# Attention, MoE and a second feed-forward layer in one program: weight conversions carried past the attention's last step

## The chip, the cores and the metric

The program runs on one core of a Trainium2 chip. The metric is the device time of one execution in microseconds; 446.7 us is the median of three runs of the kernel before (446.63 to 448.39). TensorE (PE) multiplies matrices, VectorE (DVE), ScalarE (ACT) and GpSimd (POOL) work on tiles, and SyncE (SP) issues most transfers. Each engine executes its instructions in program order. Waits between them are semaphores.

## What is computed

The reference runs three stages, one behind the other: banded attention with block summaries, a mixture of experts with one expert a token (top 1, with a capacity), and a feed-forward layer with an ELU.

```python
scores_l = scale * q @ k.T                 # masked to |i - j| < 16
scores_s = scale * q @ block_max(k).T + log(32)
a = softmax(concat(scores_l, scores_s))    # B=2, H=8, S=768, D=64
x = a @ concat(v, block_mean(v))           # -> 1536 tokens x 512

expert = argmax(x @ w_gate)                # 8 experts
h = relu(disp[expert] @ w1[expert])        # 512 -> 1024
x = gate * (h @ w2[expert])                # 1024 -> 512

h = x @ w_in                               # 512 -> 2048, w_in and w_out in float64
out = where(h > 0, h, exp(min(h, 0)) - 1) @ w_out
```

## The kernel before

**Attention.** 12 tiles of 128 tokens times two groups of heads make 24 steps, n = 0 to 23 (loop in `moe_chain_kernel`). A step runs `stage_s` (scores, L535 to L542 on PE), `stage_x` (maximum L554, negated L559 and exponentials L566), `stage_t` (transposition of the step before, L583), `stage_o` (product with v two steps back, L594, and its scaling L605). The gate of each tile (`gate_1` to `gate_6`) follows some steps behind, through the lists EARLY, MID and LATE. It ends in `put`, an indirect DMA on POOL (L718) that writes the tile's 128 rows to their expert's place in the DRAM tensor `xdisp`. The place is in `idx` (L688 on POOL, L685 on DVE for the last two tiles), of which there are two buffers. `late(n)` (L800 and on) holds what a step does besides: key windows for the next tile (`put_ks`, L450 on POOL), loads, clearing.

**Tail.** The tuple `tail` finishes the gates of the last tiles, then a few small operations make the lists of work units (`lists_i`, L990), from which SP reads addresses.

**The first unit beside it.** The first expert unit, e0, is chosen from token 0. Its 384 rows are read back early: `load_rows(XROW0)` at n = 20 (SP). The generator `first_unit` transposes them (`split_x`, four pieces of three transposes at L271, a cast on ACT at L272, a subtraction on DVE at L273), then runs 24 groups of four matmuls (L260), and then the second layer (L280). `fill_pe(n)` advances it by n pieces. `point()` reads the next entry of POINTS: the tens are pieces for `fill_pe`, the units are steps taken from `conv_tail`. `rest_of_first` runs what is left of the first unit; it starts the second layer and loads the second unit's weights and rows.

**Conversions.** w_in and w_out come as float64 in 32 chunks of 128x512 numbers (512 KB). A chunk's conversion is three DVE instructions (L405, L408, L399; called steps 1, 2 and 3 here). Chunks 8 to 13 have buffers of their own. The others, in order, share a ring of three. Step 3 of a chunk issues the load of the chunk three further on in the ring (`conv_next`), on SP's queue. Chunk 7 is loaded when chunk 4 is done, chunk 6 when chunk 3 is, 14 behind 5, 15 behind 6, 16 behind 7. In the attention, chunks 0 to 6 are queued in `pieces` from n = 10 on, one chunk every second step; `fill_in()` takes one step of them in each `stage_x` and one more in each odd `stage_o`. At n = 23 what is left in `pieces` is drained in one go (L910). Chunks 7 to 10 stand in `conv_tail`, are taken by `point()`, and what is left is drained behind the lists (L1005).

```python
            if n == NST - 1:
                while pieces:
                    fill_in()
```

Two regions of `xdisp` are cleared by SP from `fill_row`: e0's own rows at n = 8 (L840) and the spare rows behind all experts at n = 4 (L819).

Of the kernel before, what the change touches and what calls it, by code (L numbers as in the profile page):

```python
# [13 lines left out]
U32 = mybir.dt.uint32  # L14
# [12 lines left out]
E, F = 8, 1024  # L27
FF = 2048
P = 128
# [82 lines left out]
def moe_chain_kernel(  # L112
# [104 lines left out]

    puts = []
    pieces = []

    def load_rows(xr, row, queue=nc.sync):
        for s in range(NS):
# [115 lines left out]


    NCHUNK = 32  # L340
    CONV_ATT = 7
    CONV_FROM = 10
    CONV_LOAD = 7
    W_FROM = 9
    W_AT = (9, 11, 13, 15, 17, 19, 21, 23)
    X_AT = 20
    A_AT = (15, 21)
    POINTS = (0, 0, 0, 0, 11, 1, 0, 0, 30, 0, 1, 11, 0, 1, 0, 22, 0, 22, 0, 30, 10, 10, 0, 0, 10, 0, 10, 0, 0, 0, 0, 20, 40, 50)
    WARM = 23
    PROLOGUE = 2  # L350
    Y_AT = 4
    B_AFTER = (4, 7)
    H_AFTER = (0, 2, 7)
    CONV_TAIL = 4
    CONV_LATE = 3
    CONV_UNIT = (2, 8, 8)
    X_TILE = 6
# [63 lines left out]
    with ExitStack() as att:  # L421
# [105 lines left out]
        def fill_in():  # L527
            if pieces:
                pieces.pop(0)()
# [142 lines left out]
        def gate_4(i):  # L672
            gp, oh, r, s, el, nmx, xr = st.pop(("g3", i))
            rk = gp[:, E : 2 * E]
            nc.tensor.matmul(rk, tri_b, oh, start=True, stop=(i == 0))
            if i > 0:
                nc.tensor.matmul(rk, ones_b, ohs[i - 1], start=False, stop=True)
            t1, rank, row, ob = sm("t1", E), sm("rank"), sm("row"), sm("ob")
            idx = sm("idx", 1, U32)
            en = nc.vector if i >= last - 1 else nc.gpsimd  # L680
            en.tensor_scalar(row, r, -float(REG), float(E * REG), op0=ALU.mult, op1=ALU.add)
            nc.vector.scalar_tensor_tensor(t1, rk, 1.0, oh, op0=ALU.mult, op1=ALU.mult, accum_out=rank)
            en.tensor_scalar(ob, rank, cap, float(OOB), op0=ALU.is_ge, op1=ALU.mult)
            if i >= last - 1:
                nc.vector.scalar_tensor_tensor(idx, rank, row, ob, op0=ALU.add, op1=ALU.add)  # L685
            else:
                en.tensor_tensor(row, row, rank, op=ALU.add)
                en.tensor_scalar(idx, row, ob, None, op0=ALU.add)  # L688
            if i < last - 1:
                nc.scalar.activation(el, gp[:, 0:E], AF.Exp, bias=nmx, accum_out=s)  # L690
            st["g4", i] = (idx, xr, s)
# [94 lines left out]


        points = iter(POINTS)
        conv_tail = [step for i in range(CONV_ATT, CONV_ATT + CONV_TAIL) for step in conversion(i)]

        def point():
            n, conv = divmod(next(points, 0), 10)
# [5 lines left out]
        def late(n):  # L798

            i = 1 if n == 0 else (n + 3) // 2  # L800
            if (n == 0 or n % 2 == 1) and i < NTT:
                new_kw(i)
                put_ks(i, nc.gpsimd.tensor_copy)
                put_kw(i, nc.vector.tensor_copy)
            if n == 0:
                nc.sync.dma_start(wg, w_gate.rearrange("p (k e) -> p k e", e=E))
                nc.sync.dma_start(cap_raw, capacity.to_broadcast([P, 1]))
                nc.vector.tensor_copy(tri_b, C("tri"))
                nc.vector.memset(ones_f, 1.0)
            if n == 1:  # L810
                nc.gpsimd.memset(fill_row, 0.0)
                nc.gpsimd.tensor_copy(fill_row[:, DM:].bitcast(U32), C("oob").bitcast(U32))
                nc.gpsimd.tensor_copy(oobs, C("oob")[:, 0:1].bitcast(U32).to_broadcast([P, REG // P]))  # L813
                nc.vector.tensor_copy(cap, cap_raw.bitcast(I32)[:, 0:1])
            if n in (2, 4):
                load_k(1, n - 2, 2)
            if n == 4:
                nc.sync.dma_start(ids.rearrange("(p a) o -> p (a o)", a=REG // P), oobs)
                nc.sync.dma_start(xdisp[E * REG :, :].rearrange("(s p) d -> p s d", p=P), fill)  # L819
            if 5 <= n < 5 + KD:  # L820
                block_max(1, n - 5)
            if n % 2 == 0 and n // 2 + 2 < NTT:
                load_q(n // 2 + 2)
            if n % 2 == 1 and (n - 1) // 2 + 2 < NTT:
                load_vx((n - 1) // 2 + 2)
            if n in (3, 5, 6, 7):
                load_vt(1, (3, 5, 6, 7).index(n))
            if 6 <= n < 10:
                block_sums(1, n - 6, nc.gpsimd)
            if n == 11:  # L830
                block_means(vts.pop(1))
            if 11 <= n < 11 + NVX:
                put_means(n - 11)
            if n == 7:
                nc.vector.tensor_scalar(e0_i, r0[0:1], -1.0, float(E), op0=ALU.mult, op1=ALU.add)
            if n == 16:
                unit_order()
            if n == W_FROM - 1:
                e0 = st["e0"] = nc.sync.value_load(e0_i, min_val=0, max_val=E - 1)
                nc.sync.dma_start(xdisp[ds(e0 * REG, SLOT), :].rearrange("(s p) d -> p s d", p=P), fill)  # L840
            if n == W_FROM + 1:
                put(0)
            if n >= W_FROM:
                if n == X_AT:
                    nc.gpsimd.tensor_copy(oh32[:, 1], oh_x.unsqueeze(2).to_broadcast([P, E, NCH]))
                    load_rows(XROW0, st["e0"] * REG)
                load_w(st["e0"], [m for m, at in zip(W_ORDER, W_AT) if n == at])
            if n in A_AT:
                round_a(A_AT.index(n), W1_RAW[A_AT.index(n)])
            if n == CONV_LOAD:  # L850
                for m in range(len(RAW)):
                    conv_load(m)
            if n == NST - 2:
                for m in AHEAD[0:4]:
                    conv_load(m)
            if n >= CONV_FROM and conv[0] < CONV_ATT and n % 2 == 0:
                pieces.extend(conversion(conv[0]))
                conv[0] += 1
# [19 lines left out]
        for n in range(NST):  # L878
# [29 lines left out]
            if at(2):  # L908
                stage_o(*at(2))
            if n == NST - 1:  # L910
                while pieces:
                    fill_in()
            if n >= NST - 2:
                point()
            for gate, i in LATE.get(n, ()):
# [20 lines left out]
        for gate, *at in tail:  # L936
            gate(*at)
            if gate is rest_o and at[1]:
                held["acc"] = False

                for m in AHEAD[4:]:
                    conv_load(m)
            point()


# [56 lines left out]
        nc.vector.tensor_reduce(last_i[:, 0:1], got[:, 2 * MAXU : 3 * MAXU], axis=AX.X, op=ALU.max)  # L1002
        nc.vector.tensor_scalar(last_f, got[:, LAST_LIST + 1 : LAST_LIST + 2], float(2 * SLOT), float(NT), op0=ALU.is_le, op1=ALU.mult)
        nc.vector.tensor_tensor(last_i[:, 1:2], last_f, last_i[:, 0:1], op=ALU.max)
        while conv_tail:  # L1005
            conv_tail.pop(0)()

# [52 lines left out]
    def take_ids(j, xrow):  # L1062
        nc.gpsimd.tensor_copy(IT[j % 2], xrow[:, :, DM].bitcast(U32))
# [16 lines left out]

    def rest_of_first():

        while not held["second"]:
            fill_pe(1)
        take_ids(0, XROW0)
        expert = expert_of(1)
        load_w(expert, range(2))
# [4 lines left out]
        while True:  # L1092
# [8 lines left out]
            if done == NF1 - LAG - 1:  # L1101
                break
            fill_pe(1)
        for n in range(max(0, NF1 - LAG - PROLOGUE), 2):
            prologue(n)
        for f in range(NF1 - LAG, NF1 - DEFER):
# [328 lines left out]
```

## Time and profile before

| | us |
|---|---|
| median of the runs | 446.7 |
| the profiled execution, its time | 444.36 |
| its span, first to last instruction | 442.4 |
| PE busy | 415.8 (94%) |
| DVE busy | 345.2 (78%) |
| ACT busy | 233.0 (53%) |
| POOL busy | 71.7 (16%) |
| mean granted clock of PE | 0.975 |

The attention occupies the first 116 us or so, its tail and the lists run to 139 us, the expert units to 238 us, and the last layer to the end. A busy PE is not a PE at its peak, since the ends of matmuls are modelled; a stage's bound is read from what each engine waited for.

### The profile page before, as it was taken

Reading aid. Unit: us, or ns where it says so; the run is one execution under the profiler, and the core shown is the slowest. Engines: PE = TensorE matmul, PEld = TensorE weight load, DVE = VectorE, ACT = ScalarE, POOL = GpSimd, SP = SyncE. Lnnn points to the kernel's source line nnn. Section 1 sums busy time; section 2 is a strip of 40 time slices with the busy share of each in tenths; the row PEclk is TensorE's granted clock in tenths of the full one; section 3 lists DMA queues with packets and bytes.
Section 4 is the critical chain, followed back from the end, with each engine's and each line's share of the span. In section 5 each row is a group of like instructions: output and inputs, shape, how many; then the busy total and the mean of one; then the engine's idle time right before and its main releaser. Section 6 shows DMA issues by size and latency. Waiting matters only on the chain. (4 is left out here: it accounts for less than half of the span.)

```text
span 442.4 us, 8070 instructions
## 1 busy us (share of the span) xinstructions
PE 415.8 (94%) x2756; PEld 359.9 (81%) x2756; DVE 345.2 (78%) x764; ACT 233.0 (53%) x580; POOL 71.7 (16%) x147
## 2 busy tenths in 40 slices
PE   7899989996778999999999999999999999999994
PEld 4477656774778999999988997889899898998983
DVE  4568987876665968878978999999787877787871
ACT  3386778882453636356357777564434425434331
POOL 3203755732411001111000000000200000200002
PEclk9899999995799999999999999999999999999999
DMA  8959998779713798997762900020100020100001
GB/s 275 267 156 292 327 287 264 223 198 336 265 64 99 89 289 165 396 284 183 266 220 85 344 1 0 1 71 1 71 2 0 1 73 0 73 1 1 0 2 73
DMA packets 33782, 63.54 MB, mean 144 GB/s; under 512 B 5877, under 2 KB 16117, under 8 KB 33728
## 3 DMA queue, kind: packets, MB, share of 16 engines
q1 hardware_dynamic: 30320, 51.87, 41.9%
q0 software_dynamic: 3408, 11.03, 6.3%
q8 instruction: 25, 0.41, 0.5%
q14 instruction: 29, 0.24, 0.2%
HBM read 50.26 MB, written 13.42 MB: 144 GB/s over the span
## 5 line engine op out<-in xcount | busy, mean ns | idle before, releaser
L1253 PE MATMUL bank<-wout_r,hh 128*128 128x512 f32 x144 | 57.1, 396 | 1.2 <-DVE wout_r L1233 1.2
L566 ACT ACTIVATE ex<-bank,nm 128x120 f32<-128x120 f32 x96 | 33.5, 367 | 6.8 <-DVE nm L559 4.0
L1301 ACT ACTIVATE hf<-bank 128x384 f32<-128x384 f32 x24 | 11.8, 491 | 41.6 <-PE bank L260 41.6
L1253 PEld LDWEIGHTS bank<-wout_r,hh 128*128 128x128 f32 x144 | 27.1, 188 | 6.8 <-DVE wout_r L1233 2.3
L1301 ACT ACTIVATE xrow<-bank 128x384 f32<-128x384 f32 x24 | 11.7, 489 | 38.3 <-PE bank L260 38.3
L542 PE MATMUL bank<-spare,qt 64*64 64x120 f32 x384 | 26.2, 278 | 2.9 <-POOL oobs L813 1.8
L1253 PE MATMUL bank<-w2raw_r,hl 128*128 128x512 f32 x72 | 28.8, 399 | 0.0
L1253 PE MATMUL bank<-w2raw_r,hh 128*128 128x512 f32 x72 | 28.4, 394 | 0.0
L260 PE MATMUL bank<-yh,win_r 128*128 128x384 f32 x128 | 27.0, 337 | 0.0
L1265 POOL DMA_INDIRECT out_dram<-raw,idt x6 | 6.1, 1024 | 119.0 <-ACT raw L1262 117.7
L260 PE MATMUL bank<-xh,wah 128*128 128x384 f32 x112 | 25.2, 347 | 0.0
L260 PE MATMUL bank<-xh,wal 128*128 128x384 f32 x112 | 24.4, 338 | 0.5 <-DVE wal L240 0.4
L260 PE MATMUL bank<-xl,wah 128*128 128x384 f32 x112 | 24.3, 337 | 0.0
L542 PEld LDWEIGHTS bank<-spare,qt 64*64 64x64 f32 x384 | 20.5, 138 | 4.4 <-POOL oobs L813 1.9
L260 PEld LDWEIGHTS bank<-yh,win_r 128*128 128x128 f32 x128 | 22.8, 188 | 0.4
L1316 DVE SCALAR_TENSOR_TENSOR xrow<-hf,xrow 128x384 f32<-128x384 f32 x24 | 13.4, 557 | 11.2 <-ACT hf L1303 9.1
L280 PE MATMUL bank<-hh,wbh 128*128 128x384 f32 x96 | 20.9, 338 | 1.2 <-PEq L1376 0.8
L260 PEld LDWEIGHTS bank<-xh,wal 128*128 128x128 f32 x112 | 19.7, 188 | 1.3 <-DVE wal L240 1.2
L260 PEld LDWEIGHTS bank<-xh,wah 128*128 128x128 f32 x112 | 20.2, 193 | 0.6
L280 PE MATMUL bank<-hh,wbl 128*128 128x384 f32 x96 | 20.7, 337 | 0.0
L280 PE MATMUL bank<-hl,wbh 128*128 128x384 f32 x96 | 20.6, 335 | 0.0
L1316 DVE SCALAR_TENSOR_TENSOR xrow<-xrow 128x384 f32<-128x384 f32 x24 | 13.3, 556 | 9.0 <-ACT xrow L1303 9.0
(255 smaller groups left out, 1117.9 us busy)
## 6 DMA issues: line engine op xcount, KB each, us to landing
w1raw<-in_moe_w_dram SPq DMA_DIRECT2D x12, 512.0 KB, 10.1
w2raw<-in_moe_w_dram SPq DMA_DIRECT2D x12, 512.0 KB, 8.7
raw<-in_moe_w_out_dram POOLq DMA_DIRECT2D x12, 512.0 KB, 7.0
raw<-in_moe_w_in_dram SPq DMA_DIRECT2D x10, 512.0 KB, 5.7
qt<-in_q_dram SPq DMA_DIRECT2D x12, 256.0 KB, 7.8
w2raw<-in_v_dram SPq DMA_DIRECT2D x8, 384.0 KB, 9.1
rows<-in_moe_w_in_dram SPq DMA_DIRECT2D x6, 512.0 KB, 7.9
yr<-ydT SPq DMA_DIRECT2D x4, 768.0 KB, 5.0
```

The lines of the kernel that those rows point to most:

```text
L260: nc.tensor.matmul(hp, wa[a][:, kk, cols], xa[b][:, kk, :], start=(n == kk == 0), stop=(n == 2 and kk == KD - 1))
L280: nc.tensor.matmul(ACC[d][:, 0:SLOT], wb[a][:, jj, d * P : (d + 1) * P], hb[b], start=(f == 0 and n == 0), stop=(f == NF1 - 1 and n == 2),)
L542: nc.tensor.matmul(sp[j * TQ : (j + 1) * TQ, u, :], qts[i][rows, u, j * TQ : (j + 1) * TQ], kws[i][rows, u, j, :], start=False, stop=(u == 3),
L566: nc.scalar.activation(ex[:, u, :], sp[:, u, :], AF.Exp, bias=nm[:, u : u + 1], scale=0.125, accum_out=den[:, u : u + 1])
L1253: nc.tensor.matmul(ACC[s], ga[a][:, cols], wb[b][:, jj, :], start=(f == n == 0), stop=(f == NF2 - 1 and n == 2),)
L1265: put = nc.gpsimd.indirect_dma_start(out, bass.IndirectOffsetOnAxis(ap=IDT[g % 3][:, s : s + 1], axis=0), OBS[(NS * g + s) % len(OBS)], No ...
L1301: nc.scalar.activation(x, hp, AF.Relu, scale=-1.0)
L1316: nc.vector.scalar_tensor_tensor(z, x, 1.0, z, op0=ALU.add, op1=ALU.mult)
```

## The change

`conv_tail` is made at the top, so that every function sees it. At n = 23 the steps left in `pieces` are no longer drained: they are put ahead of `conv_tail`. The drain behind the lists goes. In its place `rest_of_first` takes one step after each piece of the first unit's work. One chunk fewer is queued in the attention, from n = 12 on instead of 10, and `conv_tail` holds chunks 6 to 10. The first three raw chunks are loaded at n = 9 instead of 7. The clearing of the spare rows moves from n = 4 to behind the last tile's second `rest_o`, in SP's order after the loads of chunks 12 and 13. `idx` has six buffers. In POINTS, the first piece of `split_x` moves from the end of step 22 to the tail's first entry, and the last entry takes three conversion steps besides its five pieces.

```diff
+    conv_tail = []
...
-    CONV_ATT = 7
-    CONV_FROM = 10
-    CONV_LOAD = 7
+    CONV_ATT = 6
+    CONV_FROM = 12
+    CONV_LOAD = 9
...
-    POINTS = (0, 0, 0, 0, 11, 1, 0, 0, 30, 0, 1, 11, 0, 1, 0, 22, 0, 22, 0, 30, 10, 10, 0, 0, 10, 0, 10, 0, 0, 0, 0, 20, 40, 50)
+    POINTS = (0, 0, 0, 0, 1, 1, 0, 0, 30, 0, 11, 11, 0, 1, 0, 22, 0, 22, 0, 30, 10, 10, 0, 0, 10, 0, 10, 0, 0, 0, 0, 20, 40, 53)
...
-    CONV_TAIL = 4
+    CONV_TAIL = 5
...
-            idx = sm("idx", 1, U32)
+            idx = fx.tile([P, 1], U32, tag="idx", name="idx", bufs=6)
...
-        conv_tail = [step for i in range(CONV_ATT, CONV_ATT + CONV_TAIL) for step in conversion(i)]
+        conv_tail.extend(step for i in range(CONV_ATT, CONV_ATT + CONV_TAIL) for step in conversion(i))
...
                 nc.sync.dma_start(ids.rearrange("(p a) o -> p (a o)", a=REG // P), oobs)
-                nc.sync.dma_start(xdisp[E * REG :, :].rearrange("(s p) d -> p s d", p=P), fill)
...
             if n == NST - 1:
-                while pieces:
-                    fill_in()
+                conv_tail[:0] = pieces
+                pieces.clear()
...
                 for m in AHEAD[4:]:
                     conv_load(m)
+                nc.sync.dma_start(xdisp[E * REG :, :].rearrange("(s p) d -> p s d", p=P), fill)
             point()
...
         nc.vector.tensor_tensor(last_i[:, 1:2], last_f, last_i[:, 0:1], op=ALU.max)
-        while conv_tail:
-            conv_tail.pop(0)()
...
+        def aside():
+            if conv_tail:
+                conv_tail.pop(0)()
+
         while not held["second"]:
             fill_pe(1)
+            aside()
...
             fill_pe(1)
+            aside()
+        assert not conv_tail
```

## Rows read from the trace of the kernel before

**Rows 1.** The page, part 1: busy time, share of the span, instructions.

```profile
PE 415.8 (94%) x2756; PEld 359.9 (81%) x2756; DVE 345.2 (78%) x764; ACT 233.0 (53%) x580; POOL 71.7 (16%) x147
```

**Rows 2.** Windows: busy us of PE, PEld, DVE, ACT, POOL; clock, DMA share, GB/s.

```profile
110.00:120.00 10.00, 7.12 (x51) 6.83 (x52) 7.32 (x22) 4.21 (x11) 3.46 (x8) 0.66 0.78 252
...
140.00:150.00 10.00, 10.00 (x59) 10.00 (x58) 6.67 (x11) 5.57 (x9) 0.36 (x1) 1.00 0.88 190
```

**Rows 3.** Timeline, 57 to 66 us: start, duration, engine, line, [idle before, releaser].

```profile
57.10 1.23 POOL L718 DMA_INDIRECT xdisp<-xr,idx  x1 [3.44 <-DMA spare<-in_v_dram]
...
64.59 0.84 POOL L688 TENSOR_SCALAR idx<-row,ob 128x1 uint32<-128x1 f32 x1 [2.94 <-DMA xdisp<-xr,idx]
...
65.96 1.04 PE L542 MATMUL bank<-spare,qt 64*64 64x120 f32 x16 [1.15 <-POOL spare L450]
```

**Rows 4.** Timeline of PE: first instruction of steps 14, 16 and 18.

```profile
64.30 0.36 PE L535 MATMUL bank<-masks,ident_b 128*128 128x480 bf16 x1
...
73.27 0.36 PE L535 MATMUL bank<-masks,ident_b 128*128 128x480 bf16 x1
...
80.42 0.36 PE L535 MATMUL bank<-masks,ident_b 128*128 128x480 bf16 x1
```

**Rows 5.** Timeline, 108 to 115 us: the drain at step 23 and what follows.

```profile
108.12 0.69 DVE L408 SCALAR_TENSOR_TENSOR win<-raw,win 128x512 uint32<-128x512 uint32 x1
...
111.25 0.16 DVE L682 SCALAR_TENSOR_TENSOR t<-bank,oh 128x8 f32<-128x8 f32 x1
...
111.51 0.27 ACT L690 ACTIVATE el<-bank,nmx 128x8 f32<-128x8 f32 x1 [3.48 <-DVE t L682]
...
112.88 0.51 PEld L271 LDWEIGHTS bank<-cst,rows 128*128 128x128 f32 x3 [4.22 <-DVE xl L273]
...
114.80 1.65 PE L260 MATMUL bank<-xh,wah 128*128 128x384 f32 x4
```

**Rows 6.** Timeline, 102 to 104 us; then a load's issue and its landing.

```profile
102.13 0.48 PE L271 MATMUL bank<-cst,rows 128*128 128x128 f32 x1 [1.16 <-DMA rows<-xdisp]
...
102.39 0.61 PE L535 MATMUL bank<-masks,ident_b 128*128 128x480 bf16 x1
...
103.79 0.43 DVE L405 TENSOR_SCALAR win<-raw 128x512 uint32<-128x512 uint32 x1
...
L380 SPq DMA_DIRECT2D raw<-in_moe_w_in_dram x1: 383/383/383, 98.7 to 98.7; - x1
...
DMA to landing us min/median/max: 5.1/5.1/5.1
```

**Rows 7.** Timeline, 143 to 153 us: DVE and PE in the second layer.

```profile
143.87 1.23 DVE L292 TENSOR_TENSOR wbl<-w2raw,wbh 128x1024 fp32r<-128x1024 f32 x1 [3.23 <-ACT wbh L291]
...
147.75 1.22 DVE L292 TENSOR_TENSOR wbl<-w2raw,wbh 128x1024 fp32r<-128x1024 f32 x1
...
152.50 0.94 PE L280 MATMUL bank<-hh,wbl 128*128 128x384 f32 x4
```

**Rows 8.** Timeline, 117 to 122 us: two conversion steps of the tail on DVE.

```profile
117.14 0.42 DVE L405 TENSOR_SCALAR win<-rows 128x512 uint32<-128x512 uint32 x1
...
121.92 0.69 DVE L399 SCALAR_TENSOR_TENSOR win<-rows,win 128x512 uint32<-128x512 uint32 x1
```

**Rows 9.** Landing times: one raw chunk issued at 116.4 us, four issued from 99.7.

```profile
DMA to landing us min/median/max: 3.7/3.7/3.7
...
DMA to landing us min/median/max: 7.5/8.9/10.3
```

**Rows 10.** The page, part 6: transfers from fill_row, KB, median us to landing.

```profile
xdisp<-fill_row SPq DMA_DIRECT2D x2, 774.0 KB, 10.1
...
ydT<-fill_row SPq DMA_DIRECT2D x1, 768.0 KB, 4.2
```

**Rows 11.** Timeline: the put of tile 10, and the second unit's rows read back.

```profile
129.12 0.99 POOL L718 DMA_INDIRECT xdisp<-xr,idx  x1 [7.79 <-DVE mxl L655]
...
142.53 1.44 SPq L223 DMA_DIRECT2D xrow<-xdisp  x3
```

## The prediction

> **What bounds the kernel now.** Read the page's first part, then the windows by stage, then the waits and the timeline of the stages that the change touches. PE is busy 94% of the span against DVE's 78% [rows 1], so a DVE instruction that moves is worth something only where PE stands still for it. In the window 140 to 150 us PE is busy in all ten microseconds at full clock: that stage pays for PE's work and nothing else. [...]
>
> **Index buffers and the first loads.** At 64.59 POOL has stood 2.94 us before it may write `idx`, because the put that reads the same buffer, two tiles back, had not landed. Behind that write on POOL stands `put_ks` (L450), and behind that PE, which idles 1.15 us at 65.96 for the next scores [rows 3]. With six buffers the write waits for nothing. Before it, the put at 57.10 idled 3.44 us [rows 3]; the row names a DMA that came last. The clearing of e0's rows lies in SP's order behind three raw chunks, and its landing took a median of 10.1 us with the other clearing [rows 10]; a put must not overtake it. Raw loads that follow instead of precede it let it land sooner. What all that costs is read from the steps: 16 to 18 take 80.42 - 73.27 = 7.15 us, 14 to 16 take 73.27 - 64.30 = 8.97 us [rows 4]. I take the difference, **-1.8 us**. Bounds: 0 (another input of POOL's is late in the same place) and -2.9 (all of POOL's wait at 64.59 is on the path). The three conversion steps that leave steps 11 and 12 are worth 0 here: they stand behind `nm`, so exponentials don't wait for them, and at those steps it is POOL's lateness that holds DVE; it counts below as work that comes later.
>
> **The first piece of `split_x`.** It stands ahead of step 23's scores in PE's order and waits for e0's rows: the last third is transposed at 102.13, the scores start at 102.39 [rows 6]. Moved, it lets the scores start some 2.5 us sooner. But the maximum that reads them stands in DVE's order behind two conversion steps of the tail. Those read the chunk loaded just before, issued at 98.7 and landed 5.1 us later, at 103.8; the first of them starts at 103.79 [rows 6]. In the new order these two steps belong to chunk 6, whose load is issued by chunk 3's third step; that step now falls on the slot (odd step 21) in which chunk 4's third step issued chunk 7, and SP issues it in the same place, behind `load_rows`. So the transfer becomes the wait: DVE gets to its maximum when it did before. I cost this move at **0**; bounds 0 and -2.5.
>
> **The drain at step 23.** Five conversion steps run from 108.12 to 111.25 [rows 5], 3.13 us. Behind them in DVE's order stands `t` (L682, 111.25), for which ACT idles 3.48 us, and behind ACT's `el` its casts of the transposed rows; PE idles until 112.88, 4.22 us, for DVE's subtraction [rows 5]. All of it comes 3.13 us earlier. Against that, one quarter of `split_x` more has to be cast and subtracted behind this place. From the last quarter's transposes at 112.88 to the first product at 114.80 pass 1.92 us [rows 5]; about half of it is one quarter's turn on ACT and DVE, an estimate. So **-2.1 us**; bounds -1.0 (a whole turn, and a little) and -3.1.
>
> The drained steps then take the slots of `point()`. Those hold as many steps as before, so the tail's DVE work stays the same, with other chunks in it. The drain behind the lists (one chunk) is worth 0 in itself: after it DVE idles 3.23 us for ACT at 143.87 [rows 7].
>
> **The debt.** Five steps of the drain and three from steps 11 and 12, eight in all, now run behind the lists. A chunk's steps take 0.43, 0.69 and 0.69 us [rows 5, 6], 0.60 on average: 4.8 us. One falls into DVE's idle 3.23 us; seven come between or behind the weight splits from 143.87 on, 4.2 us. What covers them is the lead of DVE over PE: the split of 147.75 ends at 148.97 and is first read at 152.50, a lead of 3.5 us [rows 7]. PE then stalls 4.2 - 3.5 = **+0.7 us**; bounds 0 (a step lies better) and +4.2 (no cover left).
>
> **The clearing of spare rows.** 774 KB, one issue on SP. At its new place SP waits with it for the puts already under way, and later puts (tiles 10 and 11) wait for it. Behind it on SP stand the load of chunk 16 and the second unit's addresses, weights and rows; behind the waiting put on POOL stand a copy into the next tile's rows, the lists' constants and a memset. A similar transfer without company lands in 4.2 us, with company in 10.1 [rows 10]. Tile 10's put starts at 129.12 and the rows are read back only from 142.53 [rows 11], so 13 us cover it. **0**; bounds 0 and +0.5, if POOL's memset comes late for the lists. At its old place the transfer held up nobody whom I can name. The load of chunk 16 now goes ahead of the second unit's weights on SP and waits for a step of the last `point()`: some 1.8 us later there (three steps), covered by the same lead.
>
> **The sum.** -1.8 + 0 - 2.1 + 0.7 = -3.2 us against the profiled execution's 444.36: 441.2 us. The median of the runs, 446.7, stands 2.3 us above that execution. I carry the difference over: **443.5 us**. Everything behind 140 us is issued by the engines' own progress, so I let the shift reach the end. This case by itself reaches from 441.5 to 445.5.
>
> **The rivals.**
>
> *The clock comes back sooner.* [...] With the drain gone PE's pause of 4.22 us [rows 5] is nearly closed. For: PE resumed at 112.88 and the clock rose soon after the first long products at 114.80. Against: these products, not the transposes, went ahead of the rise, and they still come behind the same chain. Time: 443.5 - 2.0 = 441.5 us. Chance 0.17. [...]
>
> *Gains and debt cancel.* POOL's wait is replaced by another input (0 instead of -1.8), the drain is worth its lower bound (-1.0), and one microsecond more of the debt shows (+1.7): 446.7 + 0.7 = 447.4 at the worst, about 446.5 in the middle. For: PE has a fixed amount of the first unit's work to place between 115 and 140 us, and DVE's lead is all used. Against: PE's named waits in rows 3 and 5. Chance 0.25.
>
> *Slower: chunk 7 comes late.* Its load is now issued in the tail, when chunk 4's third step has run in the slot that starts at 117.14, and its first step has the slot of 121.92 [rows 8]. DVE, in order, then stands before the last tile's scaling and the whole chain to the lists. Between the two lie 4.1 us, after the step's own time. One chunk issued at 116.4 landed in 3.7 us, one of four issued together in up to 10.3 [rows 9]. Below 4.1 us it costs nothing, at 10.3 it costs 6.2: 443.5 + 6.2 = 449.7 us. For: six chunks and puts share the engines shortly before. Against: nothing else is issued between. Chance 0.08.
>
> That the drains don't go would be seen in DVE's order; what stays of them is only the order of steps, and the second one was free.
>
> **How the numbers follow.** Forecast 0.50, clock 0.17, cancelling 0.25, slower 0.08. The predicted time is 443.5. The range leaves out the slower case and the ends of the others: 440.3 (the clock case with a microsecond more from the drain's bound) to 447.2. A measurement of this kernel tells about 0.5%, 2.2 us, from no change: faster means below 444.5, slower above 448.9. Faster: the clock case and four fifths of the forecast, 0.57. Same: the rest of the forecast and the cancelling case, 0.35. Slower: 0.08.
>
> **What would show it.** Right: no wait of POOL's `idx` for a put; steps 14 to 16 near 7.2 us; DVE idle before the first conversion step of step 22's end, up to chunk 6's landing; `t` (L682) directly behind `xt`; the first L260 about 4 us earlier than 114.8; eight conversion steps between the lists and 156 us, with PE stalls under 1 us there; the lists 4 us earlier. Wrong: step 23's maximum earlier by more than the shift (the 0 for the moved piece was wrong); a DVE wait for raw rows near 119 us; POOL waiting long before tile 10's put and DVE's list operations with it; a stall of several microseconds on PE in the second layer.

## The result: slower by 3.8 us, in a second series by 1.3 us

| | changed kernel | kernel before |
|---|---|---|
| median | 450.46 us (446.3 to 455.9, 16 runs) | 446.66 us (442.4 to 452.6, 16 runs) |
| profiled execution, span | 449.9 us, 448.3 us | 444.36 us, 442.4 us |
| mean granted clock of PE | 0.968 | 0.975 |

The ratio is 1.0086, 95% interval 1.0056 to 1.0115. In a second series (e8 below) the same kernel stood at 1.0029 (0.9995 to 1.0064), which by itself would not tell it from the kernel before. The forecast was 443.5 us with a range of 440.3 to 447.2; the time lies above it. All ratios leave out, as slow, those of a kernel's runs that lie over 1.5% above its fastest, so they can differ from the ratio of the medians (e9 below: 0.9842 from four of six runs, 0.9887 by the medians).

Helpers stand one line lower in the changed kernel (L280 is L281, L292 is L293, L405, L408, L399 are L406, L409, L400), the branch behind the first unit is L1376 instead of L1370.

**What came as forecast.** POOL's `idx` no longer waits for a put (the 2.94 us of [rows 3] have no counterpart). Steps 14, 16 and 18 start at 63.99, 71.24 and 78.39 us where [rows 4] has 64.30, 73.27 and 80.42. In the timeline of PE of the changed kernel (start, duration, engine, line, what; in brackets the idle time ahead of it and what ended it) the drain is gone: [rows 5] had an idle time of about 4 us there (4.22 for the weight loads, 3.82 for PE's products), with the first product at 114.80.

```profile
105.89 0.17 PE L676 MATMUL bank<-oh,tri_b 128*128 128x8 bf16 x1 [5.17 <-DVE oh L662]
...
108.35 0.90 PE L272 MATMUL bank<-cst,rows 128*128 128x128 f32 x3 [0.88 <-DVE xl L274]
...
111.01 1.65 PE L261 MATMUL bank<-xh,wah 128*128 128x384 f32 x4
```

The wait of 5.17 us ahead of it is the one that was expected for chunk 6, on DVE (same view):

```profile
102.38 0.43 DVE L406 TENSOR_SCALAR win<-raw 128x512 uint32<-128x512 uint32 x1 [3.95 <-DMA raw<-in_moe_w_in_dram]
...
133.83 0.23 DVE L991 TENSOR_TENSOR lists_i<-bank,cst 1x77 int32<-1x77 f32 x1 [0.47 <-PE bank L987]
```

The lists are written at 133.83 us, against 138.05 before: 4.2 us sooner, where the sum had 3.9 for that place. One pair of traces does not settle that figure. In three further traces of kernels with the same code up to there the lists came at 130.22 (e6), 133.79 (e8) and 138.43 us (e3), with the code of before at 136.64 (e4) and 138.05. They come sooner where the granted clock was higher: its mean from 110 to 120 us is 0.96 in e6, 0.87 in the changed kernel, 0.79 in e8 and 0.60 in e3. What the moves and the drain are worth is therefore read from the ratios below and not from these times.

**Where it went.** The windows of the changed kernel (busy us of PE, PEld, DVE, ACT, POOL; clock, DMA share, GB/s) show two stretches that the kernel before does not have. First the changed kernel:

```profile
140.00:150.00 10.00, 9.67 (x60) 9.40 (x59) 9.79 (x17) 6.66 (x13) 0.19 (x1) 1.00 0.82 164
150.00:160.00 10.00, 6.87 (x31) 6.24 (x30) 7.78 (x12) 1.05 (x1) 0.00 (x0) 0.85 0.87 266
...
200.00:210.00 10.00, 10.00 (x60) 10.00 (x59) 7.80 (x13) 6.52 (x11) 1.59 (x3) 1.00 0.90 51
210.00:220.00 10.00, 6.70 (x34) 6.38 (x34) 5.49 (x9) 2.41 (x4) 0.59 (x2) 0.92 0.87 319
```

Then the kernel before:

```profile
150.00:160.00 10.00, 9.68 (x61) 9.34 (x60) 7.22 (x12) 4.44 (x8) 0.00 (x0) 1.00 0.75 153
...
210.00:220.00 10.00, 9.88 (x57) 9.56 (x56) 9.76 (x15) 3.30 (x6) 1.05 (x2) 1.00 0.83 295
```

In the first, DVE has become the busy engine: 9.79 us of 140 to 150, against 6.67 in [rows 2]. The timeline of PE names the place, the branch behind the first unit; first the changed kernel, then the kernel before:

```profile
151.76 0.86 PE L281 MATMUL bank<-hl,wbh 128*128 128x384 f32 x4
153.81 0.96 PE L281 MATMUL bank<-hh,wbh 128*128 128x384 f32 x4 [1.19 <-PEq L1376]
156.71 1.47 PE L281 MATMUL bank<-hh,wbl 128*128 128x384 f32 x4 [1.94 <-DVEq L1376]
```

```profile
155.37 0.86 PE L280 MATMUL bank<-hl,wbh 128*128 128x384 f32 x4
156.55 0.95 PE L280 MATMUL bank<-hh,wbh 128*128 128x384 f32 x4 [0.32 <-PEq L1370]
157.34 0.88 PE L280 MATMUL bank<-hh,wbl 128*128 128x384 f32 x4
```

From the end of one group (152.62 and 156.23) to the start of the last row shown pass 4.09 us in the changed kernel and 1.11 before. That is 3.0 of the 4.2 us. And the last row's four products take 1.47 us, not 0.88: the mean granted clock from 156 to 162 us is 0.72, in the kernel before 1.00. The first product of the second unit then starts at 159.25, before at 158.75; the whole gain is used up.

DVE's timeline says why. [rows 7] has its two weight splits of this stretch at 143.87 and 147.75, 3.88 us apart. In the changed kernel:

```profile
139.65 1.23 DVE L293 TENSOR_TENSOR wbl<-w2raw,wbh 128x1024 fp32r<-128x1024 f32 x1 [2.88 <-ACT wbh L292]
140.80 0.55 DVE L298 TENSOR_TENSOR hl<-w1raw,hh 128x384 fp32r<-128x384 f32 x1
141.27 0.68 DVE L400 SCALAR_TENSOR_TENSOR win<-rows,win 128x512 uint32<-128x512 uint32 x1
...
147.58 1.22 DVE L293 TENSOR_TENSOR wbl<-w2raw,wbh 128x1024 fp32r<-128x1024 f32 x1
...
156.05 0.55 DVE L298 TENSOR_TENSOR hl<-w1raw,hh 128x384 fp32r<-128x384 f32 x1
```

They are 7.93 us apart: the lists came 4.2 us sooner, the second split 0.2 us sooner. And DVE still idles 2.88 us ahead of the first one, for ACT. At the second split's own operand the lead of 3.5 us was nearly enough, and PE waits a third of a microsecond:

```profile
148.86 0.98 PE L281 MATMUL bank<-hh,wbl 128*128 128x384 f32 x4 [0.33 <-DVE wbl L293]
```

What the branch waits for is DVE's last instruction ahead of it, the last row of the timeline above. Its twin in the kernel before:

```profile
156.22 0.55 DVE L297 TENSOR_TENSOR hl<-w1raw,hh 128x384 fp32r<-128x384 f32 x1
```

In the second stretch DVE waits for a raw chunk of `w_out` (changed kernel), 6.44 us where the same wait before was 1.78, and PE waits for DVE:

```profile
214.37 0.43 DVE L406 TENSOR_SCALAR wout<-raw 128x512 uint32<-128x512 uint32 x1 [6.44 <-DMA raw<-in_moe_w_out_dram]
```

```profile
217.44 0.97 PE L281 MATMUL bank<-hh,wbl 128*128 128x384 f32 x4 [3.30 <-DVE wbl L293]
```

Behind this wait, too, the clock is 0.72, from 216 to 222 us. The two profiled executions are 5.5 us apart: 0.5 us of that stands at the second unit's start, 3.3 us are this wait, and the lower clock behind it is worth up to 1.7 us (reckoned as at e12 below).

Two theories follow. **A**: the eight conversion steps come late in full at the branch, because DVE has no lead over PE there, whatever it had before. **C**: the loss is the second wait, and that wait is an accident. The rival **B**: one of the moves (loads, clearing, points) costs the time.

### The profile page after: what moved, and what is told of

Its sections match the earlier page's. It is cut to its first block, busy times and chain, and to the rows that moved or that the text cites. A ratio compares the mean times of both kernels' runs of the same rounds, so it can differ in the third digit from the quotient of the medians.

```text
span 448.3 us, 8063 instructions
## 1 busy us (share of the span) xinstructions
PE 417.8 (93%) x2756; PEld 361.8 (81%) x2756; DVE 344.3 (77%) x764; ACT 232.5 (52%) x580; POOL 72.0 (16%) x147
## 5 line engine op out<-in xcount | busy, mean ns | idle before, releaser
L1307 ACT ACTIVATE hf<-bank 128x384 f32<-128x384 f32 x24 | 11.7, 490 | 41.7 <-PE bank L261 41.7
L281 PE MATMUL bank<-hh,wbl 128*128 128x384 f32 x96 | 21.4, 346 | 5.6 <-DVE wbl L293 3.6
L261 PE MATMUL bank<-xh,wah 128*128 128x384 f32 x112 | 26.3, 359 | 0.0
L1154 ACT ACTIVATE hf<-bank 128x384 f32<-128x384 f32 x16 | 7.9, 493 | 30.1 <-PE bank L261 24.3
L281 PE MATMUL bank<-hh,wbh 128*128 128x384 f32 x96 | 20.9, 339 | 2.0 <-PEq L1376 1.2
L281 PEld LDWEIGHTS bank<-hh,wbl 128*128 128x128 f32 x96 | 17.2, 191 | 6.4 <-DVE wbl L293 4.2
L261 PEld LDWEIGHTS bank<-xh,wah 128*128 128x128 f32 x112 | 21.4, 203 | 0.6
L281 PE MATMUL bank<-hl,wbh 128*128 128x384 f32 x96 | 21.7, 350 | 0.0
```

The costliest lines, as they stand in the source:

```text
L261: nc.tensor.matmul(hp, wa[a][:, kk, cols], xa[b][:, kk, :], start=(n == kk == 0), stop=(n == 2 and kk == KD - 1))
L281: nc.tensor.matmul(ACC[d][:, 0:SLOT], wb[a][:, jj, d * P : (d + 1) * P], hb[b], start=(f == 0 and n == 0), stop=(f == NF1 - 1 and n == 2),)
L1154: nc.scalar.activation(hf, hp, AF.Relu)
L1307: nc.scalar.activation(x, hp, AF.Relu, scale=-1.0)
```

## Experiments: which part costs the time

All ratios are against the kernel before, run in the same series, with the 95% interval. Besides the series of the result there are three: e1 to e4, e5 to e8, and e9 to e12. The changed kernel itself came out at 1.0086 and 1.0029, so a difference of half a per cent between series shows little unless the traces show it too. In the expectations TensorE, VectorE, ScalarE and SyncE are PE, DVE, ACT and SP of the rows, "after" is the changed kernel and e1 to e12 are the kernels by the names given here. Those of e2 and e11 speak of four index buffers in the kernel before; it has two.

**e1, the drains put back** (index buffers, moves and points as changed).

```diff
-                conv_tail[:0] = pieces
-                pieces.clear()
+                while pieces:
+                    fill_in()
...
         nc.vector.tensor_tensor(last_i[:, 1:2], last_f, last_i[:, 0:1], op=ALU.max)
+        while conv_tail:
+            conv_tail.pop(0)()
```

> The changed kernel with both drains put back (the five pieces left in the last attention step, and what is left of the conversions behind the lists); index buffers, moved loads, moved clearing and the points stay as changed. Theory A (eight conversion steps run after the lists come 4.8 us late to the branch behind the first unit, where VectorE has no lead over TensorE): the branch is reached by VectorE before TensorE again, no 1.9 us wait of TensorE for VectorE there, and what the index buffers gain is kept: 0 to 3 us under the kernel before. Rival B (the moved loads, the clearing or the points cost the time): as slow as the changed kernel, 3 to 5 us over the kernel before. Rival C (the loss is the wait for a raw chunk at 214 us, which comes by chance of where the instruction fetch of SyncE falls): the wait at 214 us decides alone, whatever the branch does.

Measured: 0.9983 (0.9948 to 1.0019). That is clear of the changed kernel's 1.0086, but not of its 1.0029. It speaks against B, since every move is in place; B falls for good with e6, which keeps them too. Gone is also the wait for DVE at the branch: PE's waits from 140 to 162 us are a single 0.32 us, as before. DVE still waits up to 3.7 us for a raw chunk near 210 us, so C is not all of it. But of the 3 us that A left to be gained little is seen; that comes up below.

**e2, the moves undone** (drains and steps as changed).

```diff
-            idx = fx.tile([P, 1], U32, tag="idx", name="idx", bufs=6)
+            idx = sm("idx", 1, U32)
...
-    CONV_LOAD = 9
+    CONV_LOAD = 7
```

The clearing is back at step 4, too.

> The changed kernel with index buffers (four), the first raw loads (step 7) and the clearing (step 4) as before; the drains stay undone, the eight steps stay beside the second layer. Theory A: still over the kernel before, by as much as the changed kernel or up to 2 us more, since what the index buffers gave is gone but the conversion steps at the branch set the time anyway: 3 to 6 us over. Rival B: the loss is gone, within 1 us of the kernel before or faster. Rival C: depends on the wait at 214 us alone.

Measured: 1.0155 (1.0101 to 1.0210), the slowest of all. It gives no sign that the moves lose; the loss stays with the undone drains. At the branch PE waits 1.13 and 2.01 us again.

**e3, six steps moved behind the branch.**

```diff
-    CONV_UNIT = (2, 8, 8)
+    CONV_UNIT = (0, 10, 8)
```

> The changed kernel with the two conversions of the first unit (chunks 11 and 12, six steps, 3.6 us of VectorE) moved into the second unit's share: 0, 10, 8 in place of 2, 8, 8. VectorE has then two steps (1.2 us) more ahead of the branch than the kernel before, in place of eight. Theory A: TensorE's waits at the branch and behind it (4 us and the lower clock) vanish, the 4 us that are gained at the lists reach the first layer of the second unit: 2 to 4 us under the kernel before, unless the second unit is now bound by VectorE. Rival B: no change against the changed kernel, 3 to 5 us over the kernel before. Rival C: the branch's waits vanish but the time follows the wait at 214 us.

Measured: 1.0012 (0.9968 to 1.0057). Both waits at the branch are gone (0.32 us left). The time is under the changed kernel's 1.0086 but cannot be told from its 1.0029. The 2 to 4 us under the kernel before did not come: in its trace, of a run 3 us above its median, DVE waits 5.6 us in all for raw chunks between 180 and 225 us. A is right about the branch and incomplete about the rest.

**e4, the kernel before with six steps more ahead of the branch.**

```diff
-    CONV_UNIT = (2, 8, 8)
+    CONV_UNIT = (4, 6, 8)
```

> The kernel before with two conversions more (chunks 13 and 14, six steps, 3.6 us) in the first unit's share and two less in the second's: 4, 6, 8 in place of 2, 8, 8; nothing else. Theory A: VectorE comes 3.6 us late to the branch with nothing gained ahead of it: 3 to 5 us over the kernel before, and TensorE's wait there appears. Rival B and C: within 1 us of the kernel before, VectorE having room for it.

Measured: 1.0104 (1.0052 to 1.0157), 4.6 us for 3.6 us of DVE. The wait appears where it was expected, in a kernel that has nothing else of the change:

```profile
159.04 0.96 PE L280 MATMUL bank<-hh,wbl 128*128 128x384 f32 x4 [2.95 <-DVEq L1370]
```

Of 3.6 us more on DVE 2.95 come out as PE's wait, so DVE has some 0.6 us of cover at this branch in the kernel before, and no more.

## Experiments: the place of the steps

DVE's idle time ahead of its first weight split (2.88 us in the changed kernel, 3.23 in [rows 7]) was there all along. The steps beside the second layer stand behind that split in DVE's order and cannot use it.

**e5, the moves alone, in the kernel before** (the first raw loads and everything else as before).

```diff
-            idx = sm("idx", 1, U32)
+            idx = fx.tile([P, 1], U32, tag="idx", name="idx", bufs=6)
...
             if n == 4:
                 nc.sync.dma_start(ids.rearrange("(p a) o -> p (a o)", a=REG // P), oobs)
-                nc.sync.dma_start(xdisp[E * REG :, :].rearrange("(s p) d -> p s d", p=P), fill)
...
                 for m in AHEAD[4:]:
                     conv_load(m)
+                nc.sync.dma_start(xdisp[E * REG :, :].rearrange("(s p) d -> p s d", p=P), fill)
```

> The kernel before with the six index buffers and the clearing moved behind the fourteenth raw load, and nothing else of the change (drains, split of the conversions, points and first raw loads as before). Theory A, by the difference of the changed kernel with and without its moves: 2 to 3.5 us under the kernel before, no wait of TensorE at the branch behind the first unit. Rival B (these moves bring nothing without the undone drains): within 1 us of the kernel before.

Measured: 0.9945 (0.9911 to 0.9980), 2.5 us under.

**e11, the index buffers alone**: the first two lines of that edit and nothing else.

> The kernel before with six index buffers in place of four and nothing else. As predicted: 1.8 us under the kernel before (0 to 2.9), the clearing's new place adding nothing. Rival: e5's 2.5 us came from the moved clearing, and this one is within 0.7 us of the kernel before.

Measured: 0.9950 (0.9912 to 0.9988), 2.2 us (0.5 to 3.9). No gain or loss of the clearing's new place is seen; with e5 and e11 in different series, up to some 2 us either way are not excluded.

**e6, the changed kernel with its eight steps behind the lists**; `aside` then finds nothing left.

```diff
         nc.vector.tensor_tensor(last_i[:, 1:2], last_f, last_i[:, 0:1], op=ALU.max)
+        while conv_tail:
+            conv_tail.pop(0)()
```

> The changed kernel with its eight steps run in one go behind the lists, before the second layer's first split, and no step beside the second layer. Nothing is drained in the last attention step. Theory A1 (VectorE idles 3 us behind the lists, waiting for ScalarE's first rounding; five steps more there fill this idle time and leave no debt): no wait of TensorE for VectorE at the branch, and the 3 us of the undone drain are kept: 3 to 5 us under the kernel before. Rival A2 (every step that runs behind the lists is late at the branch by its own 0.6 us, wherever it stands): as slow as the changed kernel, 3 to 4 us over the kernel before, with TensorE's wait for VectorE at the branch.

Measured: 0.9931 (0.9892 to 0.9970). A2 falls, A1 holds: the same eight steps, a few microseconds sooner in DVE's order. DVE's idle time is filled (timeline of DVE of this kernel; the last conversion step, then the split):

```profile
136.78 0.69 DVE L400 SCALAR_TENSOR_TENSOR win<-rows,win 128x512 uint32<-128x512 uint32 x1
137.62 1.23 DVE L293 TENSOR_TENSOR wbl<-w2raw,wbh 128x1024 fp32r<-128x1024 f32 x1 [0.15 <-ACT wbh L292]
...
141.49 1.22 DVE L293 TENSOR_TENSOR wbl<-w2raw,wbh 128x1024 fp32r<-128x1024 f32 x1
```

In this trace the room for them is larger than in the changed kernel's, since the lists came early (130.22 us). In e7 below the lists came at 133.30 us, the last of the eight steps started at 138.32 and the split at 139.12 us: there they just fit. The splits are 3.87 us apart again. PE's waits from 140 to 162 us (for whom, us in total, times, longest), first the changed kernel, then this one:

```profile
PE bank L281 <- DVEq L1376: 1.9, 1, 1.9
PE bank L281 <- PEq L1376: 1.2, 1, 1.2
PE bank L281 <- DVE wbl L293: 0.3, 1, 0.3
```

```profile
PE bank L281 <- PEq L1378: 0.3, 1, 0.3
```

**e7 and e12, the same two places with the split of before.** Split of the conversions means which chunk runs where: the changed values of CONV_ATT, CONV_FROM, CONV_LOAD, CONV_TAIL and POINTS are the changed split, those of the kernel before the split of before. e7 is e5 with the drain of step 23 undone, its eight steps behind the lists:

```diff
-                while pieces:
-                    fill_in()
+                conv_tail[:0] = pieces
+                pieces.clear()
```

> The kernel of e5 with the drain in the last attention step undone: its five pieces go to the head of the list, one at a time beside what follows, and the eight steps that are left run behind the lists. Split of the conversions, points and first raw loads as before. Against e6 it tells what the changed split costs (VectorE waits 3.9 us for chunk 6 at 98 us in the changed kernel). Theory A1: 3 to 6 us under the kernel before. Rival A2: within 1 us of the kernel before (3 us gained at the drain, 3 us lost at the branch).

Measured: 0.9881 (0.9830 to 0.9932). A1 holds here too. e12 is e7 with these steps beside the second layer:

```diff
-        while conv_tail:
-            conv_tail.pop(0)()
...
             fill_pe(1)
+            aside()
...
             if done == NF1 - LAG - 1:
                 break
             fill_pe(1)
+            aside()
```

> The kernel of e7 with its eight steps beside the second layer, one at a time as in the changed kernel, not in one go behind the lists; nothing else. It is the cost of that place alone, without the changed split. Theory A1: six or seven of the eight steps come behind VectorE's idle time, the 4 us that they take are late in full at the branch: TensorE's waits of 1 and 2 us are there again, 3.5 to 5.5 us over e7, about 1 us under the kernel before. Prediction on record: 0.7 us over e7, since VectorE leads by 3.5 us.

Measured: 0.9991 (0.9950 to 1.0033). The place alone costs 0.9991 - 0.9881 = 1.1% of 446 us, 4.9 us, within what A1 had and seven times what the prediction had. These two stand in different series, but e6 and e8, in one series, are 1.0% apart by the same change of place. Both waits at the branch are back:

```profile
PE bank L281 <- DVEq L1376: 2.0, 1, 2.0
PE bank L281 <- PEq L1376: 1.1, 1, 1.1
...
```

Here the price can be added up. The two waits are 3.1 us, 0.3 of which stood there before: 2.8 us. And behind them the clock is low. Windows of this kernel, the first over the branch, the second behind it:

```profile
149.00:154.00 5.00, 2.68 (x14) 2.04 (x13) 5.00 (x9) 0.00 (x0) 0.00 (x0) 1.00 0.85 299
154.00:160.00 6.00, 5.18 (x21) 5.18 (x22) 1.93 (x3) 1.05 (x1) 0.00 (x0) 0.72 0.58 179
```

In the changed kernel, whose mean behind the branch is 0.72 as well, windows of one microsecond show 0.50 from 157 to 160 us and 1.00 from 161 us on. Between these two levels a mean of 0.72 in six microseconds makes 3.4 us at the lower one, so by estimate up to 1.7 us are lost. 2.8 + 1.7 = 4.5 us.

**e8, the changed kernel once more.**

> The changed kernel itself once more, for a second trace. Theory A: TensorE's waits at the branch (about 3 us together) are there again, the time is 3 to 5 us over the kernel before. Rival C: the wait of 3.3 us at 217 us is what recurs, and where it does not come the time is that of the kernel before.

Measured: 1.0029 (0.9995 to 1.0064). The waits at the branch are there again (1.1 and 2.0 us), so is one of 4.0 us for a raw chunk. The 3 to 5 us over the kernel before did not come in full: 1.3 us (-0.2 to 2.9). It is this kernel in the same series as e6, and e6 is 0.98% under it with intervals that don't meet.

## Experiments: the second wait

The wait for a raw chunk near 210 us does not come and go by chance. It goes with the changed split: its longest is 6.4 us in the changed kernel, and 3.7, 2.8, 3.8, 3.8 and 4.0 us in e1, e2, e3, e6 and e8, which have this split. With the split of before it is 1.8 us in the kernel before and 1.4, 1.2, 0.5, 0.2 and 0.3 in e4, e5, e7, e11 and e12.

Behind it PE waits for DVE in all six kernels: 3.30 us in the changed kernel, 1.63, 0.96, 1.74, 1.75 and 1.89 in e1, e2, e3, e6 and e8, and not at all at this place in the kernels with the split of before. Timeline of PE of e6:

```profile
208.16 0.96 PE L281 MATMUL bank<-hh,wbl 128*128 128x384 f32 x4 [0.71 <-DVE wbl L293]
...
211.56 0.98 PE L261 MATMUL bank<-xh,wal 128*128 128x384 f32 x4 [1.04 <-DVE wal L241]
```

What differs upstream is SyncE. It issues the last weight load (w2raw) of the third unit, then the put of that unit's row numbers (`ids`), then the loads of the rows for the next unit (`xrow`). (The expectation of e9 calls this unit the second; counted with the first unit, e0, it is the third.) The instructions of the line that issues w2raw, in the changed kernel from 186 to 199 us (count, duration in ns, first and last start):

```profile
L207 SPq EVENT_SEMAPHORE  x1: 2223/2223/2223, 188.4 to 188.4; - x1
L207 SPq MOVE w2raw<-in_moe_w_dram x1: 40/40/40, 195.7 to 195.7; - x1
L207 SPq DMA_DIRECT2D w2raw<-in_moe_w_dram x1: 386/386/386, 195.8 to 195.8; - x1
```

The wait for the buffer ends at 190.6; the next instruction comes at 195.7. The profile shows nothing that is waited for in these 5.1 us. The DMA queues of just this pause, 190.6 to 195.7 us, show a transfer of instructions on q14 (packets, MB, share):

```profile
q0 software_dynamic: 287, 1.05, 51.5%
...
q14 instruction: 1, 0.01, 0.4%
```

In the kernels with the split of before a pause of the same length (5.4 us) lies one instruction sooner, ahead of that wait, and the wait is over when SyncE gets to it. The pause keeps its place in SyncE's stream: in the traces of all kernels but e2 it follows the same number of SyncE's instructions, 309, and in e2 310. With the changed split the stream is one semaphore instruction shorter (465 against 466, e1 against e5), so a wait slips ahead of the pause. (e2 is not shorter and has the wait ahead of the pause as well; why is not shown.) So **e9**: e6 with three instructions more on SyncE, in the attention.

```diff
                 e0 = st["e0"] = nc.sync.value_load(e0_i, min_val=0, max_val=E - 1)
+                nc.sync.value_load(e0_i, min_val=0, max_val=E - 1)
```

> The kernel of e6 with one register load more on SyncE in the attention (the same value read a second time, used by nobody): three more instructions in SyncE's stream and no other work. In the traces with the changed split (after, e1, e6) SyncE waits for the buffer of the second unit's last weight load and only then, 5.1 us later, issues it, with a fetch of 8 KB of instructions in between; in before, e5 and e7 the same pause lies one instruction sooner, ahead of the wait, which is then over. Theory F (where the fetch falls decides when the row numbers of the second unit are put out, and by that the raw chunk that VectorE waits for at 205 to 215 us): the pause moves ahead of the wait, the row numbers go out 35 to 37 us behind VectorE's branch, not 41, and the time falls by 1 to 3 us against e6. Rival G: the pause is of no account, the time of e6 within 0.7 us.

Measured: 0.9842 (0.9779 to 0.9904), 0.9% under e6, 0.3% by the medians of all runs. The two intervals meet and the series differ, so the time alone does not exclude G; the trace shows what changed. The same view, from 181 to 196 us:

```profile
L207 SPq EVENT_SEMAPHORE  x3: 17/28/28, 185.5 to 185.6; - x3
L207 SPq MOVE w2raw<-in_moe_w_dram x1: 38/38/38, 185.7 to 185.7; - x1
```

On this line no instruction waits any more. `ids` goes out at 187.02, 35.4 us behind DVE's branch, not 40.9. DVE's waits for raw chunks, 180 to 225 us, first e6, then e9:

```profile
DVE wout L406 <- DMA raw<-in_moe_w_out_dram: 4.0, 2, 3.8
```

```profile
DVE wout L406 <- DMA raw<-in_moe_w_out_dram: 0.4, 1, 0.4
```

**e10, the same line more in the changed kernel.**

> The changed kernel with the same three instructions more on SyncE and nothing else. Theory A and F together: TensorE's waits of 1.1 and 2 us at the branch stay, the waits at 213 to 222 us go, 1 to 4 us under the changed kernel, so about the time of the kernel before. Rival C alone (the wait at 214 us is the whole loss): 3 to 4 us under the kernel before, as its gains ahead of the lists would be kept. Rival G: the changed kernel's time.

Measured: 0.9981 (0.9943 to 1.0018). C alone would have left 3 to 4 us of gain, and its 0.9981 is not that; A and F together are what is seen: PE's waits at the branch are still 1.1 and 2.0 us, DVE's wait for a raw chunk behind 185 us is 0.2 us, and PE's wait behind it is gone, as in e9. By the time alone G is not excluded, as the interval meets that of the changed kernel's second series.

The kernels as a table, steps by split:

| | drained as before | eight steps behind the lists | eight steps beside the second layer |
|---|---|---|---|
| split of before | 0.9945 | 0.9881 | 0.9991 |
| changed split | 0.9983 | 0.9931 | 1.0029 (first series 1.0086) |
| changed split, three instructions more | not run | 0.9842 | 0.9981 |

Between the last two columns lie 0.98 to 1.4%, 4.4 to 6.2 us, in each row; in the second and the third row both kernels stand in one series. Between the first two rows lie 0.4 to 0.5%, 1.7 to 2.2 us, in each column. Single differences of that size are within the intervals, and two of the three go across series; three of one sign stand behind it, and the traces with PE's waits, 1.63 to 1.89 us in e1, e6 and e8. How much of it SyncE's shift gives back, 0.3% or 0.9%, stays open.

## Why the prediction was wrong, step by step

- **Index buffers and first loads, -1.8 us**: right. 2.2 us for the buffers alone, 2.5 with the clearing. The moved first loads were not tried by themselves.
- **First piece of `split_x`, 0**: right to half a microsecond, and for the reason given: DVE idles 3.95 us up to chunk 6's landing. Step 18 came 2.0 us sooner, step 23's maximum 1.6 us sooner (103.46, before 105.03).
- **Drain at step 23, -2.1 us**: right. Drained against behind the lists: 0.64% and, across series, 0.52%; 2.9 and 2.3 us. PE's idle time fell from 3.82 to 0.88 us. The 4.22 us that the prediction gives for PE are those of the weight loads; the sum does not use them.
- **Clearing of spare rows, 0**: nothing speaks against it (0.9945 against 0.9950). Tile 10's put moved to 130.27 us, 1.15 us later where the work around it came 4 us sooner, and nothing waited for it.
- **The debt, +0.7 us**: this is the step that failed; 4.4 to 6.2 us, 4.9 with the split of before. The count was right: eight steps, one of them in DVE's idle time and seven behind the first split. The cover was wrong. The lead of 3.5 us was read at one split [rows 7], 152.50 - 148.97, and taken to hold for the stretch. It belongs to that operand, and there it held: PE waited 0.33 us. At the end of the stretch the branch has next to none: in the kernel before DVE finished its last `hl` at 156.77 us, 0.5 us behind PE's last product ahead of the branch (156.23) and 0.6 us ahead of the product that has to wait in the changed kernel (157.34). The cover of a debt is the smallest lead up to the point where the two engines meet next, and here that is 0.6 us. Some 3 us came out as PE's waits, within the bound of +4.2 us (no cover left); the clock behind them, up to 1.7 us, stood in neither bound.
- **"Everything behind 140 us is issued by the engines' own progress, so I let the shift reach the end"**: wrong. SyncE's pause falls behind one of its waits and no longer ahead of it. That delays the put of the third unit's row numbers and the row loads behind it, and costs 1.7 to 2.2 us. Nothing in the prediction looked at how long SyncE's stream becomes.
- **The rivals.** Whether the clock comes back sooner is not settled: in 110 to 120 us its mean rose from 0.66 [rows 2] to 0.87 in the changed kernel and the lists came as the sum had it without this gain, but in kernels with the same code up to there it lies between 0.60 and 0.96, and the lists move with it. No run shows the 2.0 us in this rival's time; what the traces show is a clock of 0.50 until 116.5 us and of 1.00 from 117 us on in the kernel before, and, with the means of 0.60 (e3) and 0.96 (e6), lists at 138.43 and 130.22 us. Chunk 7 did not come late: between 104 and 134 us DVE waits 0.2 us in all for raw chunks. "Gains and debt cancel" had the right mechanism, DVE's lead all used up, with one microsecond of debt where it was over four; its other two conditions, no gain from the buffers and the lower bound at the drain, did not come.

With the measured sizes (the middles of 2.3 and 2.9, 4.4 and 4.9, 1.7 and 2.2) the sum is -2.2 - 2.6 + 4.7 + 2.0 = +1.9 us, between the two series' 1.3 and 3.8.

## What to carry to other kernels

Work that is put off is paid where the two engines meet next, with the smallest lead on the way and not the one that is easiest to read; look for that point, here a branch, and read both engines' last instruction ahead of it. Work moved out of a busy place belongs ahead of the next wait of its engine, not behind it: the same eight steps cost 4.4 to 6.2 us where seven of them stand behind an idle time of 3 us, and left PE 0.3 us of waiting at the branch (e6, e7) where all stand ahead of it. With the steps there the change is worth it: 0.9881 (0.9830 to 0.9932) with the split of before, 0.9931 with the changed split, 0.9842 (four runs, 0.9887 by all six) with SyncE's stream shifted as well.

## What the runs showed of the hardware

**SyncE's instruction stream has a pause of some 5 us.** SyncE stood still for 5.0 to 5.4 us in thirteen of the fourteen traces, and for 3.6 us in e3, with no semaphore wait that the profile shows. In four of these pauses (changed kernel, before, e6, e9) the DMA engines were 78 to 106% busy by the sum of their queues' shares, and a transfer of instructions fell into each: one packet on q14, 0.4% of the 16 engines' time, which makes some 0.3 us on one of them in 5.1 to 5.3 us. Three more instructions (e9) moved the pause ahead of a wait that was over when the pause ended. Two branches of SyncE's lie 0.3 us ahead of it in the kernel before; whether the transfer of instructions, one of these branches or the busy DMA engines make it so long was not tried.

**Reading rows back keeps the DMA engines busy at a low rate.** Once the rows of the next unit are loaded (`xrow`, 384 rows of 2,064 bytes), the engines are busy and move little. Windows of the changed kernel, where `ids` is issued at 197.03 and the rows from 199.26:

```profile
200.00:204.00 4.00, 4.00 (x25) 4.00 (x24) 3.93 (x8) 2.85 (x5) 0.53 (x1) 1.00 1.01 35
204.00:208.00 4.00, 4.00 (x25) 4.00 (x24) 3.87 (x6) 3.03 (x5) 0.53 (x1) 1.00 0.88 34
208.00:212.00 4.00, 4.00 (x25) 4.00 (x24) 0.00 (x0) 1.60 (x3) 0.53 (x1) 1.00 0.88 263
```

A share of about 1 at 35 GB/s, then 263. The DMA queues from 200 to 208 us (packets, MB, share) show who it is:

```profile
DMA packets 141, 0.27 MB, mean 34 GB/s; under 512 B 8, under 2 KB 8, under 8 KB 141
...
q1 hardware_dynamic: 141, 0.27, 94.8%
```

Only 8 of these packets are small; the others are rows, which took 406 ns each on average from 196 to 212 us, while the weight load's packets of 2,048 bytes took 106 ns. The small elements of `ids` had moved before 200 us. A raw chunk issued into the first of these windows, at 200.52, landed 13.8 us later; that is the one DVE waits for. Why a row takes so long was not tried.

**PE's clock is low behind the waits at the branch.** Two waits of PE within 4.1 us, 1.1 to 1.2 and 1.9 to 2.0 us, are followed by a mean granted clock of 0.72 over the next six microseconds, in the changed kernel in both series and in the three other kernels that have both waits. It is 0.72 as well in e4, with waits of 0.3 and 2.95 us, and 1.00 in the other eight kernels, with a single 0.32 us at that place.
